# The first x tiles by transposing loads, and one gate earlier in TensorE's order, in a gated mix of two attention blocks

## The chip, the cores and the metric

The kernel runs on one core of a Trainium2 chip. The metric is the device time of one execution in microseconds (us), lower is better; three executions were timed and their median counts.

## The reference

One input x (2048 positions by 1024 features, bfloat16) goes through two attention blocks A and B, each with 32 heads of 32 features and its own weights, and the two results are mixed by a gate:

```python
g = sigmoid((x * gate_w).sum(-1, keepdims=True))
qkv = x @ wqkv                       # per block
# A: linear attention
pq, pk = phi(q), phi(k)              # phi(t) = where(t > 0, t + 1, exp(t)) + 1e-6
o = (pq @ (pk.T @ v)) / (pq @ pk.sum(positions) + 1e-6)
# B: each position attends to 8 positions, itself and 7 before it, 2 apart
o = softmax(q . k[pos - 2 w] / sqrt(32)) @ v[pos - 2 w],  w = 0..7
out = g * (oA @ A_wo) + (1 - g) * (oB @ B_wo)
```

B's own x is not used; both blocks read A's.

## The kernel before

**Tiles and pairs.** The positions are split into the even and the odd ones, 1024 each, since B looks back in steps of two. Each half has 8 row tiles of 128 positions, so there are tiles 0 to 15. A *pair* is two tiles of the same half, four apart: pair 0 is tiles 0 and 4, pair 1 tiles 1 and 5, pair 2 tiles 2 and 6, pair 3 tiles 3 and 7; pair 4 is tiles 8 and 12, pair 5 tiles 9 and 13, and so on (`tile_of`). x is needed with its features on the partitions, as `xT`.

**Products.** Most projections are made by a *group* (class `Group`): two row tiles by 1024 columns as a two by two block product with seven block products in place of eight (`m1` to `m7`). Each block product is a run of 128x128 by 512 matmuls in one line, L264; the operands that are sums of blocks are made beforehand on VectorE (DVE): `Weights.sums` (L131 to L134) for weights, `xsums` (L100 to L103) for x, the last of which overwrites a part of xT in place. ScalarE (ACT) copies partial results out of PSUM (L273), DVE adds them (L246).

**Queues.** The order of TensorE (PE) and of SyncE (SP), which issues nearly all loads and stores, is the order of the program text; ACT and DVE are ordered by a scheduler. SP issues its transfers one behind the other, and a store waits there until what it stores has been written.

**The start.** B's values come first, because attention reads them back from DRAM (`V_d`). The loads in SP's order: tile 0 of x plainly, into `xr` (L191), three of the four quarter loads of the first 512 columns of B's value weights `W` (`vb_load`, L184; the first quarter goes over ACT's queue), tile 4 of x plainly, tiles 1 and 5 by a transposing load straight into xT (`xt_load`, L90), the four quarters of the second 512 columns, then tiles 2, 6, 3 and 7 by transposing loads. All loads named here have 256 KB.

Meanwhile PE runs 14 matmuls on a zeroed tile (`warm_up`, L467), whose result nothing reads. `vb_plain(0, 1)` then makes the values of pairs 0 and 1 with ordinary products, tiles in the order 0, 4, 1, 5: eight matmuls (L520, psum tile K) over the eight feature chunks for the first 512 columns of each tile, and then the second 512 columns of all four. Before tile 0's first matmul stand the eight PE transposes of tile 0 (L476, with an identity `ident` built on GpSimd (POOL)), and before its seventh those of tile 4; ACT and DVE each copy half of the result into xT (L478).

After each tile's first half stands its `gate` (L456): eight matmuls of xT with one column, gate_w, into one column of the psum tile `gps`. `gate` for pairs 2 to 7 stands at written places between groups. All sixteen columns must be there at `gate_end`, which comes behind gates(6, 7) and value group 4.

Behind the plain products the program reads as follows (value groups of pairs 2 to 5 are `vb_group`; `run` issues a group; `defer` and `later` put work a number of products later):

```python
    vb_plain(0, 1)
    x_loads(4, 5)
    ws, xs = wvB.sums(), xsums(2)
    gates(2)
    ...
    later(2, lambda: gates(3))
    run(lambda: vb_group(2), 0)
    x_loads(6, 7)
    run(lambda: vb_group(3), 0)
    gates(4, 5)
    run(lambda: vb_group(4), 0)
    gates(6, 7)
    gate_end()
```

`x_loads(4, 5)` issues the transposing loads of tiles 8, 12, 9 and 13 on SP; ahead of them in SP's queue stand the four stores of V for pairs 0 and 1 (L502), each of which waits for ACT's last casts of these values. Value group 3 reads pair 3, value group 4 reads pair 4.

**The rest** (from about 47 us on) is the k and q groups, attention of B in pieces as side work between the products, A's k and v groups, A's q products with the linear attention, and the output products.

Of the kernel before, what the change touches and what calls it, by code (L numbers as in the profile page):

```python
# [9 lines left out]
ALU = mybir.AluOpType  # L10
AX = mybir.AxisListType
BF16 = mybir.dt.bfloat16
FP16 = mybir.dt.float16
F32 = mybir.dt.float32
P = 128
# [11 lines left out]
def kernel(  # L27
# [11 lines left out]
    nc = tc.nc  # L39
    ctx.enter_context(tc.manual_schedule(engines={mybir.EngineType.PE, mybir.EngineType.SP}))  # L40
    x = A_x[0]
    S, D = x.shape
# [10 lines left out]
    def xrows(t):  # L53
        return xpar[t // 8, (t % 8) * P:(t % 8 + 1) * P, :]

    consts = ctx.enter_context(tc.tile_pool(name="consts", bufs=1))
# [7 lines left out]
    ering = ctx.enter_context(tc.tile_pool(name="ering", bufs=4))  # L64
    smallp = ctx.enter_context(tc.tile_pool(name="smallp", bufs=4))
    ofp = ctx.enter_context(tc.tile_pool(name="ofp", bufs=3))
    ps_pj = ctx.enter_context(tc.tile_pool(name="ps_pj", bufs=1, space=bass.MemoryType.PSUM))
# [13 lines left out]
    xT = [xp.tile([P, 8, 2, 512], BF16, name="xT", tag=f"x{p}") for p in range(2)]  # L81
# [5 lines left out]
    def xt_load(t):  # L87
        p, j = divmod(t, 8)
        hf, c = divmod(j, 4)
        nc.sync.dma_start_transpose(out=xT[p][:, :, hf, c * P:(c + 1) * P], in_=xrows(t))  # L90

    def xsums(pair):
        p, c = divmod(pair, 4)
        sl = slice(c * P, (c + 1) * P)
        a11, a21 = xT[p][:, 0:4, 0, sl], xT[p][:, 0:4, 1, sl]
        a12, a22 = xT[p][:, 4:8, 0, sl], xT[p][:, 4:8, 1, sl]
        s1, s2, s4 = (SS[p][:, k, :, sl] for k in range(3))
        s3 = xT16[p][:, 0:4, 1, sl]
        tt = nc.vector.tensor_tensor
        return [lambda: tt(out=s1, in0=a21, in1=a22, op=ALU.add),  # L100
                lambda: tt(out=s2, in0=s1, in1=a11, op=ALU.subtract),
                lambda: tt(out=s4, in0=a12, in1=s2, op=ALU.subtract),
                lambda: (tt(out=s3, in0=a11, in1=a21, op=ALU.subtract), ready.add(pair))]  # L103
# [55 lines left out]
    def col_weights(src, col0, nn, pool=None):  # L159
# [3 lines left out]
        for j in range(2):  # L163
# [8 lines left out]
    W = wp.tile([P, 8, D], BF16, name="W", tag="W")  # L172
    T = tp.tile([P, 3, 4, 512], FP16, name="T", tag="T")
    T3v = kqp.tile([P, 4, 512], FP16, name="T3v", tag="kq")
    bview = B_wqkv.rearrange("(k p) n -> p k n", p=P)
    ident = consts.tile([P, P], BF16, name="ident")
    nc.gpsimd.memset(ident[:], 0.0)
    nc.gpsimd.affine_select(out=ident[:], in_=ident[:], compare_op=ALU.not_equal, fill=1.0, base=0,
                            pattern=[[1, P]], channel_multiplier=-1)
    gw = consts.tile([P, 8], BF16, name="gw")  # L180
    nc.gpsimd.dma_start(out=gw[:], in_=gate_w.rearrange("(k p) -> p k", p=P))

    def vb_load(k, j, q=nc.sync):
        q.dma_start(out=W[:, 2 * k:2 * k + 2, 512 * j:512 * j + 512],  # L184
                    in_=bview[:, 2 * k:2 * k + 2, 2 * D + 512 * j:2 * D + 512 * j + 512])

    xr = {}

    def xr_load(t):
        xr[t] = ering.tile([P, D], BF16, name="xr", tag="e")  # L190
        nc.sync.dma_start(out=xr[t][:], in_=xrows(t))  # L191
    vb_load(0, 0, nc.scalar)
    xr_load(0)
    vb_load(1, 0)
    vb_load(2, 0)
    vb_load(3, 0)
    xr_load(4)
    for t in (1, 5):
        xt_load(t)
    for k in range(4):  # L200
        vb_load(k, 1)
# [4 lines left out]
    def x_loads(*pairs):  # L206
        for pair in pairs:
            for i in range(2):
                xt_load(tile_of(pair, i))
# [30 lines left out]
    last_dve = [None]  # L240
# [154 lines left out]
    def defer(products, ops, gap=1):  # L395


        deferred.append([state["now"] + products, list(ops), gap])
# [3 lines left out]
    def later(products, f):  # L402
        tasks.append([state["now"] + products, f])
# [23 lines left out]
    def run(make, rate, *after, last=False):  # L427


        g, p = make(), state["prev"]  # L430
        g.after = after
        g.last = last
        for q, f in [(g, g.m1), (g, g.m2)] + ([(p, p.m3)] if p else []) + [(g, g.m6)] \
                + ([(p, lambda: end_of(p))] if p else []) + ([(g, g.m5), (g, g.m7)] if last else [(g, g.m7), (g, g.m5)]):
            f()
            side(rate, q.nk // 4)
        state["prev"] = g
# [7 lines left out]
    def tile_of(pair, i):  # L445
        return (pair // 4) * 8 + (pair % 4) + 4 * i
# [5 lines left out]
    def gate(t):  # L452
        p, j = divmod(t, 8)
        hf, c = divmod(j, 4)
        for kc in range(8):
            nc.tensor.matmul(gps[:, t:t + 1], lhsT=xT[p][:, kc, hf, c * P:(c + 1) * P], rhs=gw[:, kc:kc + 1],  # L456
                             start=kc == 0, stop=kc == 7)
# [7 lines left out]
    def warm_up(n):  # L465
        for _ in range(n):
            nc.tensor.matmul(gps_tile[:, 1, 0:256], lhsT=warm[:, 0:P], rhs=warm, start=True, stop=True)  # L467

    def transpose(t):
        p, j = divmod(t, 8)  # L470
        hf, c = divmod(j, 4)
        for k0, tag, copy in ((0, "X1", nc.scalar.copy), (4, "Y1", nc.vector.tensor_copy)):
            tps = ps_pj.tile([P, 512], F32, name="tps", tag=tag)
            tps = tps.bitcast(BF16)[:, 0:512].rearrange("p (k n) -> p k n", k=4)
            for k in range(4):
                nc.tensor.transpose(tps[:, k, :], xr[t][:, (k0 + k) * P:(k0 + k + 1) * P], ident[:])  # L476
            with tc.high_priority():
                last_dve[0] = copy(out=xT[p][:, k0:k0 + 4, hf, c * P:(c + 1) * P], in_=tps).ins  # L478


    def v_tiles(name):
        if name == "va":
            return [tring.tile([P, H, 32], BF16, name=name, tag="t") for _ in range(2)]
        vs = [tring.tile([P, H, 33], BF16, name=name, tag="t") for _ in range(2)]
        for v in vs:
            nc.gpsimd.memset(v[:, :, 32:33], 1.0)  # L486
        return vs

    def v_final(vs, by_chunk=False):
        def final(i, j, ps, add):  # L490
            if by_chunk:
                out_ = vs[i][:].rearrange("p (c a h) e -> p a c h e", c=4, a=2)[:, j, :, :, 0:32]
                rs = lambda ap: ap.rearrange("p (c h e) -> p c h e", c=4, e=32)
            else:
                out_ = vs[i][:, 16 * j:16 * j + 16, 0:32]
                rs = lambda ap: ap.rearrange("p (h e) -> p h e", e=32)
            acc(out_, rs(ps), None if add is None else rs(add))
        return final

    def vb_store(vs, pair, i):  # L500
        t = tile_of(pair, i)
        nc.sync.dma_start(out=V_d[t // 8][(t % 8) * P:(t % 8 + 1) * P, :],  # L502
                          in_=vs[i][:].rearrange("p h e -> p (h e)"))
# [5 lines left out]
    def vb_plain(*pairs):  # L509


        vs = {pair: v_tiles("va") for pair in pairs}
        tiles = [(pair, i) for pair in pairs for i in range(2)]

        def ps_of(pair, i):
            return ps_pj.tile([P, 512], F32, name="K", tag="XY"[i] + str(pair % 2))

        def mm(ps, pair, i, j, kc):
            p, c = divmod(pair, 4)
            nc.tensor.matmul(ps[:], lhsT=xT[p][:, kc, i, c * P:c * P + P],  # L520
                             rhs=wvB.W[:, kc, 512 * j:512 * j + 512], start=kc == 0, stop=kc == 7,
                             skip_group_check=True)
        for pair, i in tiles:
            ps = ps_of(pair, i)
            for kc in range(8):
                if (pair, i) == tiles[0] and kc in (0, 6):
                    transpose(tile_of(pair, kc // 6))
                mm(ps, pair, i, 0, kc)
            gate(tile_of(pair, i))
            v_final(vs[pair], True)(i, 0, ps[:], None)  # L530
        tiles = tiles[2:] + tiles[:2]
        ps = {t: ps_of(*t) for t in tiles}
        for k in range(4):
            for t in tiles:
                for kc in (2 * k, 2 * k + 1):
                    mm(ps[t], *t, 1, kc)
                if k == 3:
                    pair, i = t
                    v_final(vs[pair], True)(i, 1, ps[t][:], None)
                    vb_store(vs[pair], pair, i)  # L540
# [312 lines left out]
        return Group(operands, final, nk=8, scale=sc)  # L853


    warm_up(14)

    wkB, wqB, wqA = {}, {}, {}

# [10 lines left out]
    def load_q(nn, delay=8):  # L870
        return load_col(wqB, B_wqkv, 0, nn, delay=delay)
# [4 lines left out]
    def gates(*pairs):  # L876
        for pair in pairs:
            for i in range(2):
                gate(tile_of(pair, i))
    vb_plain(0, 1)  # L880
    x_loads(4, 5)
    ws, xs = wvB.sums(), xsums(2)
    gates(2)
    with tc.issue_after(last_dve[0]):
        for f in (ws[0], ws[1], xs[0], xs[1], ws[2], xs[3], ws[3], xs[2]):
            f()
    later(2, lambda: gates(3))
    defer(2, xsums(3) + xsums(0))
    run(lambda: vb_group(2), 0)
    x_loads(6, 7)  # L890
    defer(1, xsums(4) + xsums(1))
    run(lambda: vb_group(3), 0)
    load_k(0, 13)()
    load_q(0, 20)()
    gates(4, 5)
    defer(2, xsums(5))
    run(lambda: vb_group(4), 0)
    gates(6, 7)
# [101 lines left out]
```

## Time and profile before

| | |
|---|---|
| median of 3 executions | 460.67 us (460.46 to 460.70) |
| the profiled execution, its own time | 460.67 us |
| its span in the trace, first to last instruction | 458.9 us |
| mean granted clock of TensorE | 0.999 |
| PE busy | 446.0 us, 97% of the span |
| PE weight loads, DVE, ACT, POOL busy | 216.0, 282.9, 237.1, 60.8 us |
| moved by DMA | 51.61 MB |

All places in time are microseconds from the span's start. A row of the timeline has start, duration, engine, line, operation, output and inputs with shapes, and how many instructions were merged into it; in brackets, how long the engine was idle before it, and what ended that. "SPq" is SP's queue: the duration there is that of issuing, not of the transfer. "To landing" is from the start of issuing until the transfer's semaphore tells of its end. Matmuls are pipelined: a 512-column one is shown with 379 ns while the next one starts 216 ns later.

### The profile page before, as it was taken

Reading aid. Unit: us, or ns where it says so; the run is one execution under the profiler, and the core shown is the slowest. Engines: PE = TensorE matmul, PEld = TensorE weight load, DVE = VectorE, ACT = ScalarE, POOL = GpSimd, SP = SyncE. Lnnn points to the kernel's source line nnn. Section 1 sums busy time; section 2 is a strip of 40 time slices with the busy share of each in tenths; the row PEclk is TensorE's granted clock in tenths of the full one; section 3 lists DMA queues with packets and bytes.
Section 4 is the critical chain, followed back from the end, with each engine's and each line's share of the span. In section 5 each row is a group of like instructions: output and inputs, shape, how many; then the busy total and the mean of one; then the engine's idle time right before and its main releaser. Section 6 shows DMA issues by size and latency. Waiting matters only on the chain.

```text
span 458.9 us, 11765 instructions
## 1 busy us (share of the span) xinstructions
PE 446.0 (97%) x5070; PEld 216.0 (47%) x5070; DVE 282.9 (62%) x452; ACT 237.1 (52%) x345; POOL 60.8 (13%) x119
## 2 busy tenths in 40 slices
PE   6999999998999999999999999999999999999996
PEld 3455444444444444444445444445554444444444
DVE  0456768669748387484774846669777973256112
ACT  2234357557476484673855847536676544222221
POOL 8100000000000000000000000007686313000000
PEclk9999999999999999999999999999999999999999
DMA  8899911790301703007030066391229772695111
GB/s 219 149 227 246 297 18 71 204 193 3 99 4 38 155 1 101 1 26 165 5 98 4 24 135 189 109 244 47 71 74 216 169 172 91 146 219 129 48 46 46
DMA packets 111955, 51.61 MB, mean 112 GB/s; under 512 B 75552, under 2 KB 107552, under 8 KB 111904
## 3 DMA queue, kind: packets, MB, share of 16 engines
q1 hardware_dynamic: 111600, 50.61, 46.2%
q8 instruction: 39, 0.64, 0.6%
q10 hardware_dynamic: 272, 0.26, 0.2%
q14 instruction: 12, 0.10, 0.1%
q0 software_dynamic: 32, 0.00, 0.1%
HBM read 26.22 MB, written 16.78 MB: 94 GB/s over the span
## 4 chain that ended last, share of the span: by engine, by line
PE 90%; ACT 6%; DMA 1%; DVE 0%; SPq 0%; issue 0%; ACTq 0%; DVEq 0%
PE X L264 42%; PE Y L264 28%; PE Q L661 9%; PE K L520 3%; ACT PT L701 3%; PE o L712 2%; PE oA L618 2%; ACT eA L545 2%; PE s L696 1%; DMA xr<-in_A_x_dram 1%; PE kps L579 1%; ACT tA L244 1%; PE o L717 1%; PE Y L299 1%; ACT U2s L273 1%; PE gps L456 1%
## 5 line engine op out<-in xcount | busy, mean ns | idle before, releaser
L264 PEld LDWEIGHTS <-xT 128*128 128x128 bf16 (+1 forms) x352 | 33.0, 98 | 39.6 <-issue 1.8
L264 PE MATMUL X<-T,SS 128*128 128x512 f16 x176 | 45.3, 380 | 0.7 <-ACT U2s L273 0.7
L264 PEld LDWEIGHTS <-WS 128*128 128x128 bf16 (+1 forms) x288 | 28.1, 98 | 33.6
L661 PE MATMUL Q<-xT,WS 128*128 128x512 bf16 x192 | 43.7, 379 | 0.0
L264 PE MATMUL X<-SS,TS 128*128 128x512 f16 x144 | 37.0, 379 | 3.9 <-ACT U2s L273 3.9
L273 ACT COPY U4s<-X 128x512 f32<-128x512 f32 x40 | 23.4, 584 | 32.9 <-PE X L264 32.8
L486 POOL MEMSET vA<- 128x32 bf16 x16 | 4.0, 250 | 268.3 <-DVE eA L548 144.9
L264 PE MATMUL Y<-W,xT 128*128 128x512 bf16 (+1 forms) x152 | 39.0, 379 | 0.0
L264 PEld LDWEIGHTS <-SS 128*128 128x128 f16 x264 | 24.3, 98 | 29.7 <-issue 2.8
L701 ACT ACTIVATE PT<-s 128x2048 bf16<-128x2048 f32 x16 | 29.9, 1869 | 15.1 <-PE s L696 15.0
L264 PE MATMUL Y<-xT,WS 128*128 128x512 bf16 (+1 forms) x144 | 37.0, 379 | 0.0
L264 PEld LDWEIGHTS <-TS 128*128 128x128 f16 x216 | 20.5, 98 | 29.0 <-issue 5.9
L702 DVE TENSOR_TENSOR PT<-PT,maskp 128x2048 bf16<-128x2048 bf16 x16 | 19.6, 1224 | 22.1 <-ACT PT L701 22.1
L273 ACT COPY M1s<-X 128x512 f32<-128x512 f32 x40 | 23.6, 589 | 11.5 <-PE X L264 10.4
L661 PEld LDWEIGHTS <-WS 128*128 128x128 bf16 x192 | 18.3, 98 | 20.1
L273 ACT COPY U2s<-X 128x512 f32<-128x512 f32 x40 | 23.3, 583 | 8.2 <-PE X L264 8.2
L264 PEld LDWEIGHTS <-oT 128*128 128x128 bf16 (+1 forms) x176 | 17.2, 98 | 20.5
L629 POOL TENSOR_TENSOR obA<-ofv,rec 128x512 bf16<-128x512 f32 x22 | 25.7, 1187 | 0.9
L724 DVE COPY nB<-o 128x1024 f32<-128x1024 f32 x16 | 19.5, 1220 | 6.0 <-ACT rB L723 6.0
L723 ACT ACTIVATE rB<-o 128x1024 f32<-128x1024 f32 x16 | 16.4, 1025 | 12.3 <-DVE oB L730 9.5
L264 PE MATMUL X<-W,xT 128*128 128x512 bf16 x88 | 22.7, 380 | 0.0
L264 PE MATMUL X<-T,oS 128*128 128x512 f16 x96 | 22.7, 379 | 0.0
(140 smaller groups left out, 766.7 us busy)
## 6 DMA issues: line engine op xcount, KB each, us to landing
V_d<-va SPq DMA_DIRECT2D x16, 256.0 KB, 3.1
WS<-in_B_wqkv_dram SPq DMA_DIRECT2D x16, 256.0 KB, 4.2
W<-in_A_wqkv_dram SPq DMA_DIRECT2D x8, 512.0 KB, 6.0
vw<-V_d SPq DMA_DIRECT2D x16, 256.0 KB, 4.3
OB_d<-oB SPq DMA_DIRECT2D x16, 256.0 KB, 2.2
OA_d<-obA SPq DMA_DIRECT2D x16, 256.0 KB, 2.3
out_dram<-osb SPq DMA_DIRECT2D x30, 128.0 KB, 1.8
oT<-OB_d SPq DMA_DIRECT2D x12, 256.0 KB, 3.9
```

The costliest lines, as they stand in the source:

```text
L264: nc.tensor.matmul(ps[:], lhsT=lhsT, rhs=rhs, start=start and kc == 0, stop=kc == self.nk - 1, skip_group_check=True)
L273: nc.scalar.copy(out=s[:], in_=ps[:])
L520: nc.tensor.matmul(ps[:], lhsT=xT[p][:, kc, i, c * P:c * P + P], rhs=wvB.W[:, kc, 512 * j:512 * j + 512], start=kc == 0, stop=kc == 7, ski ...
L545: nc.scalar.activation(out=e, in_=t, func=ACT.Exp)
L618: nc.tensor.matmul(o[:, k, 132 * j:132 * j + 132], lhsT=es[i][:, j, k * P:(k + 1) * P], rhs=KVz[:, nn + 4 * j, :], start=True, stop=True)
L629: nc.gpsimd.tensor_tensor(out=ob[:, k:k + 2], in0=of[:, k:k + 2, :, 0:32], in1=rec[:, k:k + 2].broadcast_to([P, 2, 8, 32]), op=ALU.mult)
L661: nc.tensor.matmul(ps[:], lhsT=w.W[:, kc, j * P:j * P + P], rhs=xT[p][:, kc, i, :], start=kc == 0, stop=kc == 7, skip_group_check=True)
L701: nc.scalar.activation(out=PT[:], in_=s[:], func=ACT.Exp, scale=SCALE)
L702: nc.vector.tensor_tensor(out=PT[:], in0=PT[:], in1=maskp[:, None, :].broadcast_to([P, 4, 512]), op=ALU.mult)
L712: nc.tensor.matmul(o[32 * g:32 * g + 32, 2 * b, cols], lhsT=vw[rows, j, 4 * ch + g, :], rhs=PT[rows, g, cols], start=True, stop=True)
L723: nc.scalar.activation(out=rB[:], in_=o[:, 1:4:2, :], func=ACT.Ln)
L724: nc.vector.tensor_copy(out=nB[:], in_=o[:, 0:4:2, :])
```

## The change

Four edits, all in the first 35 us:

1. Tiles 0 and 4 of x are loaded by transposing loads straight into xT, as the others are. Tile 0's goes first on SP, tile 4's follows the three weight quarters. `transpose`, `xr`, the identity on POOL, 16 PE transposes and 4 copies on ACT and DVE go.
2. `warm_up` has 24 matmuls in place of 14 at the start, and three more stand before the third, fifth and seventh matmul of tile 0.
3. The sums for group 2 on DVE are no longer ordered behind the last copy of the transposes. DVE's order there becomes: first, second and third weight sum, first sum of x, fourth weight sum, the other three sums of x. Before, it was: first weight sum, first sum of x, second weight sum, second sum of x, third and fourth weight sum, and the last two sums of x.
4. `gates(4)` moves from behind value group 3 to ahead of it; `gates(5)` stays behind it.

Everything else has the same instructions in the same order on every engine and queue. Nothing of attention is in the diff.

```diff
-    ident = consts.tile([P, P], BF16, name="ident")
-    nc.gpsimd.memset(ident[:], 0.0)
-    nc.gpsimd.affine_select(out=ident[:], in_=ident[:], compare_op=ALU.not_equal, fill=1.0, base=0,
-                            pattern=[[1, P]], channel_multiplier=-1)
...
-    vb_load(0, 0, nc.scalar)
-    xr_load(0)
-    vb_load(1, 0)
-    vb_load(2, 0)
-    vb_load(3, 0)
-    xr_load(4)
-    for t in (1, 5):
+    vb_load(0, 0)
+    xt_load(0)
+    for k in range(1, 4):
+        vb_load(k, 0)
+    for t in (4, 1, 5):
         xt_load(t)
...
-    def transpose(t):
-        p, j = divmod(t, 8)
-        hf, c = divmod(j, 4)
-        for k0, tag, copy in ((0, "X1", nc.scalar.copy), (4, "Y1", nc.vector.tensor_copy)):
-            tps = ps_pj.tile([P, 512], F32, name="tps", tag=tag)
-            tps = tps.bitcast(BF16)[:, 0:512].rearrange("p (k n) -> p k n", k=4)
-            for k in range(4):
-                nc.tensor.transpose(tps[:, k, :], xr[t][:, (k0 + k) * P:(k0 + k + 1) * P], ident[:])
-            with tc.high_priority():
-                last_dve[0] = copy(out=xT[p][:, k0:k0 + 4, hf, c * P:(c + 1) * P], in_=tps).ins
...
-                if (pair, i) == tiles[0] and kc in (0, 6):
-                    transpose(tile_of(pair, kc // 6))
+                if (pair, i) == tiles[0] and kc in (2, 4, 6):
+                    warm_up(3)
                 mm(ps, pair, i, 0, kc)
...
-    warm_up(14)
+    warm_up(24)
...
-    with tc.issue_after(last_dve[0]):
-        for f in (ws[0], ws[1], xs[0], xs[1], ws[2], xs[3], ws[3], xs[2]):
-            f()
+    for f in (ws[0], ws[1], xs[0], xs[1], ws[2], xs[3], ws[3], xs[2]):
+        f()
...
     run(lambda: vb_group(2), 0)
     x_loads(6, 7)
+    gates(4)
     defer(1, xsums(4) + xsums(1))
     run(lambda: vb_group(3), 0)
     load_k(0, 13)()
     load_q(0, 20)()
-    gates(4, 5)
+    gates(5)
```

More of the change, by code (lines that the diff above doesn't have):

```diff
@@ L175, with vb_load @@
     bview = B_wqkv.rearrange("(k p) n -> p k n", p=P)
-    ident = consts.tile([P, P], BF16, name="ident")
-    nc.gpsimd.memset(ident[:], 0.0)
-    nc.gpsimd.affine_select(out=ident[:], in_=ident[:], compare_op=ALU.not_equal, fill=1.0, base=0,
-                            pattern=[[1, P]], channel_multiplier=-1)
     gw = consts.tile([P, 8], BF16, name="gw")
     nc.gpsimd.dma_start(out=gw[:], in_=gate_w.rearrange("(k p) -> p k", p=P))
[L183 to L191, printed above, removed]
-    vb_load(0, 0, nc.scalar)
-    xr_load(0)
-    vb_load(1, 0)
-    vb_load(2, 0)
-    vb_load(3, 0)
-    xr_load(4)
-    for t in (1, 5):
+    def vb_load(k, j):
+        (nc.scalar if (k, j) == (0, 0) else nc.sync).dma_start(out=W[:, 2 * k:2 * k + 2, 512 * j:512 * j + 512],
+                          in_=bview[:, 2 * k:2 * k + 2, 2 * D + 512 * j:2 * D + 512 * j + 512])
+    vb_load(0, 0)
[3 more added lines that the diff above has]
+    for t in (4, 1, 5):
         xt_load(t)
```

## The prediction

> **What bounds the kernel now.** The page first: it says which engine sets the time.
>
> ```profile
> PE 446.0 (97%) x5070; PEld 216.0 (47%) x5070; DVE 282.9 (62%) x452; ACT 237.1 (52%) x345; POOL 60.8 (13%) x119
> PE   6999999998999999999999999999999999999996
> ```
>
> TensorE (PE) is busy 97% of the span; only the first and the last of the 40 slices show holes. So every microsecond by which PE's stream starts later, or stands still, is a microsecond of the time. The chain of waits, cut to the start, shows what holds PE there (start, duration, what):
>
> ```profile
> 2.67 6.10 DMA xr<-in_A_x_dram
> 8.77 0.05 issue
> 8.82 0.62 PE tps L476 x8
> 9.44 0.43 PE K L520 x2
> 9.87 0.18 PE gps L456 x8
> 10.05 1.75 PE K L520 x8
> ```
>
> The chain runs through the load of row tile 4 (issued 2.67, landed 8.77), its eight transposes, the last two matmuls of tile 0, tile 0's gate, and then PE without a break. The timeline gives PE's start instruction by instruction (start, duration, and in brackets the idle time before it and what ended it):
>
> ```profile
> 1.20 3.05 PE L467 MATMUL gps<-KVacc 128*128 128x256 bf16 x14 [1.20 <-DVE KVacc L170]
> 4.16 0.62 PE L476 MATMUL tps<-ident,xr 128*128 128x128 bf16 x8
> 5.23 1.04 PE L520 MATMUL K<-W,xT 128*128 128x512 bf16 x4 [0.45 <-ACT xT L478]
> 6.99 0.59 PE L520 MATMUL K<-W,xT 128*128 128x512 bf16 x2 [0.72 <-DMA W<-in_B_wqkv_dram]
> 8.82 0.62 PE L476 MATMUL tps<-ident,xr 128*128 128x128 bf16 x8 [1.24 <-DMA xr<-in_A_x_dram]
> ```
>
> Tile 4's first matmul starts at 9.91, which is 1.14 us after its load landed. Next the same view of SP, the queue that issues the loads:
>
> ```profile
> 0.74 0.39 SPq L191 DMA_DIRECT2D xr<-in_A_x_dram  x1
> 1.19 1.44 SPq L184 DMA_DIRECT2D W<-in_B_wqkv_dram  x3
> 2.67 0.47 SPq L191 DMA_DIRECT2D xr<-in_A_x_dram  x1
> 3.18 5.33 SPq L90 DMA_TRANSPOSE xT<-in_A_x_dram  x2
> 24.18 11.99 SPq L90 DMA_TRANSPOSE xT<-in_A_x_dram  x8
> ```
>
> The eight transposing loads from 24.18 on are those of pairs 4 to 7; the first two are tiles 8 and 12, which make pair 4. Last, PE around the place to which the change moves pair 4's gate:
>
> ```profile
> 24.92 0.54 PE L456 MATMUL gps<-gw,xT 128*128 128x1 bf16 x16
> 25.33 1.02 PE L264 MATMUL X<-T,SS 128*128 128x512 f16 x4
> 27.05 1.03 PE L264 MATMUL X<-T,SS 128*128 128x512 f16 x4
> 27.91 1.03 PE L264 MATMUL X<-W,xT 128*128 128x512 bf16 x4
> 33.96 0.94 PE L456 MATMUL gps<-gw,xT 128*128 128x1 bf16 x32
> 34.76 1.02 PE L264 MATMUL X<-W,xT 128*128 128x512 bf16 x4
> ```
>
> and the landing of tile 12, from the answer for its line cut to its one issue, at 25.56:
>
> ```profile
> DMA to landing us min/median/max: 4.2/4.2/4.2
> ```
>
> The same answer for tile 8, issued at 24.18, has 4.5. So tile 8 lands at about 28.7 and tile 12 at 25.56 + 4.23 = 29.79.
>
> **Part 1, gates(4) moved.** PE takes its instructions in the written order. The change puts the 16 gate matmuls of pair 4 ahead of value group 3, whose first matmul runs at 27.91. They read tiles 8 and 12, which are not there until 28.7 and 29.79. In the kernel before, the same 16 stood behind group 3 at 33.96, four microseconds after both had landed, and waited for nothing. Queued behind them is all of PE, and behind PE the evictions of ACT and DVE and V's stores on SP. Nothing covers it. The price: PE comes to gate(8) near 27.9, waits for 28.7, does it, waits for 29.79, does gate(12), and goes on. Eight weight loads with eight narrow matmuls that nothing could prefetch take about 0.40 us (the load rows of gate(0): it starts at 9.49, the next matmul's load at 9.89). Group 3 starts at 29.79 + 0.04 + 0.40 = 30.23, that is 2.32 late. What is saved at the old place: 32 gate matmuls take 33.96 to 34.76 = 0.80 there, 16 take 24.92 to 25.33 = 0.41, so 0.39 comes off. **Net +1.93 us.** Both sides move with PE, for the loads of pair 4 are issued behind V's first four stores, which wait for casts that follow PE. An earlier or later start therefore doesn't change this stall. Bounds: with the quickest landing among the 14 such loads (4.1) it is +1.8; with the slowest (6.5) +4.2. I take 4.23, the row of this very load.
>
> Would the stall be given back? Behind 35 us the chain is PE with short stretches of ACT and DVE, all set off by PE itself; no DMA stands in it that a late PE would find ready. So it stays.
>
> **Part 2, the start.** Two plain loads of x (tiles 0 and 4) with 16 PE transposes, 2 ACT copies (0.59 each) and 2 DVE copies (0.42 each) go; two transposing loads come. What counts is when tile 4's matmuls start, 9.91 before; from there on PE's order is the same up to the gates of part 1. Gone is the 1.14 us between tile 4's landing and its first matmul. Against it the loads: the plain transfers between 4.11 (tile 0's load landed; PE's weight load for its first transpose starts at 4.15) and 8.77 are five of 256 KB, 0.93 us each. The eight transposing loads of 256 KB land from 24.18 + 4.5 to 34.28 + 4.1, seven gaps in 9.7 us, 1.38 each. So each exchange costs 0.45: tile 4 lands at 8.77 + 0.90 = 9.67. Further, the first of them holds SP 1.45 us (the first of the two from 3.18) in place of 0.39, so the weight loads are issued 1.06 later. That costs nothing as long as the DMA engines have work, and 1.06 if they run dry. Their busy share by microsecond (windows of the trace) is 0.26 from 1 to 2, 0.73 from 2 to 3 and 0.83 or more from there to 10, so I take 0.2, near the lower end. Tile 4 lands at 9.87 and its matmul starts at 9.92. **Net 0.0 us**, bounds -0.2 and +0.9 from the issue alone.
>
> The Trainium skill, page "Advanced Engine Details and Errata", section X-Bar Transpose (TRN2), says that transposing DMAs are as fast as ordinary ones. The rows above say otherwise (1.38 against 0.93); by the rule alone tile 4 would land at 8.77, the start come 1.1 us sooner, and the time be 461.5.
>
> With nothing of PE's to hide: the 24 warm-up matmuls. 14 took 3.05 us (218 ns each for 256 columns, half the later rate of 216 ns for 512), so ten more end between 5.3 and 6.5. From the late end, 8 matmuls (1.73), nine more warm-ups at the later rate (0.97) and the gate (0.2) end at 9.4, before tile 4 is there. They are hidden with 0.5 us to spare, and would show were tile 4 to land at 8.8.
>
> **Edits without a price.** Tiles 1 and 5 land at 11.25 and 12.6; needed at 11.85 and 13.8. The second half of the weights follows by 0.93 steps (13.6 to 16.4), needed from 15.7 to 20.9; tiles 2, 6, 3, 7 by 21.9, the last needed at 24.7. The tightest is tile 1 with 0.6. On POOL the identity (0.21 + 0.30) goes, and the gate vector's load is issued half a microsecond sooner. On DVE two of the three weight sums that stood behind the wait for tile 6 now stand ahead of it; the last of this group of sums ended at 23.70 and PE loads its result at 25.97, so nothing moves there. On SP one of the three transposing loads that now follow each other will be held as tile 5's is (5.33 for the two from 3.18, so 3.88 for the second), and the second half of the weights, queued behind it, is issued up to 2 us later: near 10.5, which with the 3.2 us that its first load took to land is 13.7 again. The attention code is the same on both sides of the diff.
>
> **The sum.** The profiled execution took 460.67 (span 458.9, and 1.8 around it) and is also the median. 460.67 + 1.93 + 0.0 = **462.6 us**. About 0.2% (0.9 us) is what a measurement of this kernel can tell from no change.
>
> **Rivals.**
> Transposing loads that cost no more than plain ones here (10%): tile 4 lands at 8.77 and its matmul starts at 8.82, 1.09 sooner; the stall stays: 460.67 + 1.93 - 1.09 = 461.5, within the 0.2%; a late end of the warm-ups would take back up to 0.6. For it: tile 1 (3.18 + 6.5) landed only 0.9 behind tile 4. Against: the 1.38 of eight in a row.
>
> Late start (9%): tile 0's load, now the first and a transposing one, takes 6.5 us from its issue as tiles 1 and 5 did, lands at 7.24 instead of 4.11, and all behind it slips: tile 4 at 7.24 + 4.66 + 0.45 = 12.35, the start +2.5, the time up to 465.1. Against: tiles 1 and 5 had six and seven loads ahead of them.
>
> The clock falls back (7%). In the stall PE is idle some 0.8 and 0.9 us; the start has short waits too. If the rate halves as in the first 3.05 us, half of that, 1.5 us, is lost: 464.1. Against: 1.24 us of idle time before 8.82, after which the matmuls ran at 216 ns each. The Trainium skill, "TensorE: Matmul & The Clock Gate", Part 1, puts the idle window after which the rate halves at about 3.4 us; no row here shows a wait that long.
>
> Faster (4%): the start comes forward by more than the gates cost. To be faster by 0.9 the first matmul of tile 4 would have to come at 9.91 - 1.93 - 0.92 = 7.06, so tile 4 land by 7.0, where before even the plain load landed at 8.77. At a landing of 6.5 the time is 459.2. Only a DMA queue that runs much quicker without the plain x loads does that, and no row shows one.
>
> **How the numbers follow.** The forecast has 70%. Slower by over 0.2%: 70 + 9 + 7 = 86%; same 10%; faster 4%. The range goes from the case of quick transposes, 461.5, to the forecast with the clock's loss or a late start, with some room for a slower landing in the stall: 464.7.
>
> **What would show it.** Right: in the timeline after, the gate's row behind group 2 has idle time of 1.5 to 2 us in front, ended by a DMA of xT; value group 3 starts 2.3 late against tile 4's start; the later gate row has 16 matmuls; PE's order and gaps behind it are as before. Tile 4's first matmul stands between 9.7 and 10.8. Wrong: no wait there (tiles 8 and 12 landed early), or a start that moves by more than a microsecond, or new waits at tiles 1 and 5.

## The result and the profile after

The changed kernel took 462.98 us (median of 4 executions, 462.49 to 463.25), the kernel before 460.69 (4 executions, 460.46 to 461.02): a ratio of 1.0048, 95% interval 1.0031 to 1.0065. The change makes the kernel slower, by 0.3 to 0.65%. The profiled execution after took 463.25, with a span of 461.5 against 458.9 before.

The page of the changed kernel, lines of busy time and of PE's 40 slices:

```profile
PE 448.1 (97%) x5073; PEld 217.6 (47%) x5073; DVE 282.4 (61%) x450; ACT 235.9 (51%) x343; POOL 59.4 (13%) x117
PE   8989999998999999999999999999999999999996
```

PE has 3 matmuls more (19 warm-ups came, 16 transposes went) and is still the bound. The first slice fills (6 to 8), the third falls from 9 to 8: a slice is 11.5 us, and the third holds the moved gate.

The chain of waits after, cut to the first 36 us (start, duration, what):

```profile
3.90 5.75 DMA xT<-in_A_x_dram
9.64 0.05 issue
9.69 1.90 PE K L497 x8
...
23.96 1.35 SPq L90
25.36 4.19 DMA xT<-in_A_x_dram
29.55 0.05 issue
29.60 0.35 PE gps L444 x8
29.95 0.89 PE X L252 x4
```

There are now two loads in it. The first is tile 4's, at the same place as before: landed at 9.64, first matmul 0.05 later. The second is new: tile 12's, which lands at 29.55 and releases its gate, and behind it value group 3. The timeline of PE shows both stretches (start, duration, what; in brackets the idle time in front). First the start:

```profile
1.20 4.85 PE L455 MATMUL gps<-KVacc 128*128 128x256 bf16 x24 [1.20 <-DVE KVacc L170]
5.89 0.59 PE L497 MATMUL K<-W,xT 128*128 128x512 bf16 x2
6.32 0.49 PE L455 MATMUL gps<-KVacc 128*128 128x256 bf16 x3
7.30 0.59 PE L497 MATMUL K<-W,xT 128*128 128x512 bf16 x2 [0.49 <-DMA W<-in_B_wqkv_dram]
9.25 0.34 PE L444 MATMUL gps<-gw,xT 128*128 128x1 bf16 x8
9.69 1.90 PE L497 MATMUL K<-W,xT 128*128 128x512 bf16 x8
```

Tile 4 starts at 9.69 against 9.91: 0.22 sooner. The only wait of note ahead of it is 0.49 for a weight quarter. Then the gate:

```profile
26.84 1.03 PE L252 MATMUL X<-T,SS 128*128 128x512 f16 x4
28.58 0.35 PE L444 MATMUL gps<-gw,xT 128*128 128x1 bf16 x8 [0.70 <-DMA xT<-in_A_x_dram]
29.60 0.35 PE L444 MATMUL gps<-gw,xT 128*128 128x1 bf16 x8 [0.67 <-DMA xT<-in_A_x_dram]
29.82 1.02 PE L252 MATMUL X<-W,xT 128*128 128x512 bf16 x4
35.85 0.54 PE L444 MATMUL gps<-gw,xT 128*128 128x1 bf16 x16
36.26 1.02 PE L252 MATMUL X<-W,xT 128*128 128x512 bf16 x4
```

Two waits on xT, one for each tile of pair 4. Value group 3 starts at 29.82 in place of 27.91, and value group 4, behind the now shorter gate row, at 36.26 in place of 34.76. So 1.50 us of the loss stand at 36 us: 1.72 for the gate, less 0.22 from the start.

The span, however, is 2.6 us longer. The other 1.1 come late, where both kernels have the same program. Half of it shows at one place, in B's attention; the row of the kernel before, then that of the changed one:

```profile
289.95 0.22 PE L712 MATMUL o<-PT,vw 64*32 64x56 bf16 x8 [0.32 <-issue]
```

```profile
292.00 0.23 PE L689 MATMUL o<-PT,vw 64*32 64x57 bf16 x11 [0.89 <-issue]
```

PE waits here for nothing that the trace shows, 0.32 us in one profile and 0.89 in the other. At this place, between the products `o` and the next group's, the profiles of the experiments below have 0.23 to 1.78, among them 0.40 (gate put back), 0.71 (gate two products later), 0.67 (the changed kernel again), 1.33 (gate put back, fewer warm-ups) and 1.78 (the kernel before with the extra warm-ups). So the gap varies from profile to profile, and it can be wide without the moved gate. That coming late widens it is not ruled out: it is at most 0.71 in the six profiles in which PE gets there before 290.6 us, and 0.46 to 1.78 in the eight in which it gets there later. The second profile of the changed kernel lost 1.90 by group 4 and 2.2 in its whole span (461.1 against 458.9). What sets these late increments was not found.

Some executions of several kernels, the kernel before among them (17 of 93), have a mean granted clock under 0.998 and take some 2 us longer; below they are said to have lost clock, and their share is given where it matters.

### The profile page after: what moved, and what is told of

The parts are those of the page before. It is cut to its first block, busy times and chain, and to the rows that moved or that the text cites. A ratio compares the mean times of both kernels' runs of the same rounds, so it can differ in the third digit from the quotient of the medians.

```text
span 461.5 us, 11765 instructions
## 1 busy us (share of the span) xinstructions
PE 448.1 (97%) x5073; PEld 217.6 (47%) x5073; DVE 282.4 (61%) x450; ACT 235.9 (51%) x343; POOL 59.4 (13%) x117
## 4 chain that ended last, share of the span: by engine, by line
PE 85%; ACT 6%; DMA 3%; SPq 2%; POOL 1%; DVE 1%; issue 1%; ACTq 0%; DVEq 0%; POOLq 0%
PE X L252 39%; PE Y L252 26%; PE Q L638 9%; ACT PT L678 3%; PE K L497 2%; PE o L689 2%; DMA xT<-in_A_x_dram 2%; ACT eA L522 2%; PE s L673 1%; PE oA L595 1%; PE kps L556 1%; DMA oT<-OA_d 1%; ACT tA L232 1%; POOL obA L606 1%; PE o L694 1%; PE Y L287 1%
```

## The experiments

The theory: the loss is the wait of pair 4's gate for tiles 8 and 12; the new start is even. The rivals: the start has a price of its own (transposing loads, warm-ups); or the granted clock falls in the waits.

### The two halves of the change

**The changed kernel with the gate put back** behind value group 3:

```diff
     x_loads(6, 7)
-    gates(4)
...
-    gates(5)
+    gates(4, 5)
```

> The changed kernel with pair 4's gate back behind value group 3 (gates(4, 5) there); its start stays as changed. Theory (the wait at the moved gate is the whole loss, the start is even): no wait of PE for a load of xT around 27.7, value group 3 starts at 27.7 (0.2 before that of the kernel before), time 460.4 to 460.7. Rival (the new start or what follows from it costs something late in the kernel, where the changed kernel's profile has about 1.1 us more than the moved gate explains): 461.0 to 461.8, with the surplus after 285 us.

Measured: 461.13 us (460.85 to 461.61, 12 executions) against 461.24 for the kernel before on the same chip (32 executions); ratio 0.9984, interval 0.9969 to 1.0000. The start by itself is even or a trifle quicker: of its 12 executions none lost clock, where 7 of the 32 of the kernel before did, and the other 25 of these have a median of 461.14. The time is above the 460.4 to 460.7 that I expected, and so is that of the kernel before on this chip.

**The kernel before with the gate ahead alone**, the other half:

```diff
     x_loads(6, 7)
+    gates(4)
...
-    gates(4, 5)
+    gates(5)
```

> The kernel before with pair 4's gate alone moved ahead of value group 3; the start stays as before. Theory: the whole loss is here, PE waits twice for loads of xT (together 1.3 to 1.5 us of idle matmul time), value group 4 starts 1.7 to 1.9 late, time 462.4 to 463.0. Rival (the start has part of the loss): under 462.0.

Measured: 465.50 us (462.37 to 466.99, 9 executions), ratio 1.0062 (1.0032 to 1.0092). By the median this is more than the changed kernel lost, and more than expected. Four executions that kept their clock have a median of 463.33, 2.2 over those of the kernel before (461.14); the other five, at 465.50 to 466.99, lost clock as well. The profiled execution is one of these. Its PE timeline at tile 4's transposes and around the gate:

```profile
9.74 1.03 PE L476 MATMUL tps<-ident,xr 128*128 128x128 bf16 x8 [2.24 <-DMA xr<-in_A_x_dram]
30.78 0.35 PE L456 MATMUL gps<-gw,xT 128*128 128x1 bf16 x8 [0.39 <-DMA xT<-in_A_x_dram]
32.64 0.35 PE L456 MATMUL gps<-gw,xT 128*128 128x1 bf16 x8 [1.51 <-DMA xT<-in_A_x_dram]
32.86 1.49 PE L264 MATMUL X<-W,xT 128*128 128x512 bf16 x4
```

and its windows (stretch, its length, PE's busy time and instructions, granted clock, DMA share, GB/s):

```profile
8.00:12.00 4.00, 2.25 (x19) 0.67 1.03 189
12.00:16.00 4.00, 3.95 (x29) 0.90 1.09 302
32.00:36.00 4.00, 3.14 (x16) 0.66 1.10 204
36.00:40.00 4.00, 4.00 (x19) 0.91 1.38 175
```

The clock is granted at 0.66 in the four microseconds of the gate's wait and after, and group 3's first four matmuls take 1.49 us where they took 1.02 or 1.03. So the rival of the clock is a thing that happens, at the gate and, in the first two rows, at the start of this old kernel too. There the wait was for tile 4: its plain load landed at 9.70 in this profile, not at 8.77, and PE stood idle for 2.24 us ahead of its transposes.

**The kernel before with a plain delay** of 18 warm-up matmuls at the gate's new place, and no gate moved. It asks whether a loss of 2 us at this place is given back:

```diff
     x_loads(6, 7)
+    warm_up(18)
```

> The kernel before with 18 matmuls of 256 columns on a zeroed tile, whose result nothing reads, put ahead of value group 3, where the changed kernel has the moved gate: PE is late by 18 x 0.108 = 1.94 us with no wait for a load. Theory (a delay of PE there is passed on to the end, one for one): 460.7 + 1.9 = 462.4 to 462.8. Rival one (the later kernel gives some of it back): under 462.2. Rival two (being late costs more, at the instruction supply near 290 and the loads of the output stage near 350): 463.1 to 463.8.

Measured: 465.02 us (463.17 to 467.29, 12 executions), ratio 1.0065 (1.0041 to 1.0089). In its profile the delay is as set: the row starts at 30.63, group 3 at 32.59, 1.96 later. Of the 12 executions 7 kept their clock, with a median of 463.86, 2.7 over the kernel before; nothing of the delay is given back. My 462.4 to 462.8 was missed, for no execution is under 463.17; the second rival, that being late costs more than the delay itself, is nearer. Of the places that it names, the gap near 290 us is 0.77 in this profile for 0.32 before. Why it is 2.7 and not 2.0, and why 5 of 12 lost clock though the delay itself leaves PE no idle time, this run doesn't tell; in its profile the clock fell at the start (0.74 and 0.83 in the stretches from 8 to 16 us), where PE had waited 2.17 us for tile 4's load.

### Is the wait the price, or the place?

**The changed kernel with the gate two products later**, inside value group 3, where PE comes when the tiles are about to be there:

```diff
-    gates(4)
+    later(2, lambda: gates(4))
```

> The changed kernel with pair 4's gate two products later, behind the second product of value group 3 instead of ahead of the group; the gate is neither back in its old place nor ahead. Theory (the cost is the landing of tile 12 less the time at which PE comes there): PE comes at 29.4 and tile 12 lands at 29.6 to 30.2, so 0 to 0.7 us of waiting are left in place of 1.9; median 461.0 to 461.6. Rival (the place itself costs, whatever PE's time there): 462.5 or more.

**The changed kernel as it is**, on the same chip:

> The changed kernel as it is, beside the others on the same chip, for the granted clock over more executions. Theory: the start keeps the clock (nothing under 1.00 in 8 to 16 us), the two waits of together 1.4 to 2 us at the moved gate halve it in some executions, which then cost 1 to 2 us more than the others; median 462.8 to 464. Rival (only the start's waits touch the clock): all within 462.4 to 463.4.

Measured: 461.05 us (460.56 to 462.25, 12 executions) for the later gate, ratio 0.9991 (0.9977 to 1.0005); 462.99 (462.42 to 464.85, 8 executions) for the changed kernel, ratio 1.0044 (1.0024 to 1.0064); the kernel before 461.40 on this chip. Two products, 1.7 us of PE's time, take away 1.94 us. PE's rows at the gate, with the gate two products later:

```profile
28.75 1.03 PE L252 MATMUL Y<-W,xT 128*128 128x512 bf16 x4
29.62 0.65 PE L444 MATMUL gps<-gw,xT 128*128 128x1 bf16 x16
30.13 1.02 PE L252 MATMUL X<-W,SS 128*128 128x512 bf16 x3
```

No idle time is left in front of the 16 gate matmuls. The price was PE's arrival against the landing; the early place has no other that could be measured. In the changed kernel's second profile the waits are 0.29 and 1.20, group 3 starts at 30.21, and the loss at group 4 is 1.90, of which 0.08 is the start. Three of its 8 executions lost clock (3 of 12 with the four of the result), where none of the 24 with the same start and without the wait did.

**The changed kernel with the gate's waits filled** by warm-up matmuls, so that PE isn't idle there:

```diff
-    gates(4)
+    warm_up(7)
+    gate(tile_of(4, 0))
+    warm_up(7)
+    gate(tile_of(4, 1))
```

> The changed kernel with 7 warm-up matmuls of 0.11 us each ahead of tile 8's gate and 7 between it and tile 12's gate, so that PE works for about 1.5 us of its two waits. Theory (the waits set the place of group 3, and their idle time is what halves the clock in some executions): median as the clock-intact runs of the changed kernel, 462.7 to 463.1, and none at 464.5 or with a mean clock under 0.997. Rival (the clock is lost elsewhere): some still there.

Measured: 463.85 us (462.49 to 464.90, 10 executions), ratio 1.0049 (1.0032 to 1.0065). No execution lost clock, against 3 of 8: that points the expected way, on small numbers. The median is above what was expected: 2.5 over the kernel before on its chip, where the changed kernel without these fillers has 1.6 on another. The ratios, 1.0049 and 1.0044, are not apart. Its profile was a late one: pair 4's loads were issued from 24.50 on in place of 23.96, a wait of 0.23 was left ahead of tile 8's gate, group 4 started at 37.15 in place of 36.26, and the late gap is 1.28. As a remedy for the gate's wait it saves nothing, since the landing stays where it is.

### The start: what the warm-ups are worth

**The changed kernel with the 14 warm-ups of before** and without the triples:

```diff
-                if (pair, i) == tiles[0] and kc in (2, 4, 6):
-                    warm_up(3)
...
-    warm_up(24)
+    warm_up(14)
```

> The changed kernel with 14 warm-up matmuls in place of 24, and none between tile 0's matmuls. Theory (hidden behind the loads): tile 4's first matmul still at 9.6 to 9.8, matmuls at 216 ns from there, time as the changed kernel, 462.7 to 463.3. Rival (the extra warm-ups hold the matmul rate up over the waits): tile 4's and tile 1's matmuls at up to 430 ns, up to 1.5 us more, 464 to 464.5.

Measured: 464.60 us (462.92 to 466.59, 12 executions), ratio 1.0054 (1.0035 to 1.0074); 7 of the 12 lost clock. My expectation was wrong, the rival's right: in the profile tile 4's eight matmuls run at half rate, behind a wait of 1.69 us for the weights.

```profile
9.93 3.29 PE L497 MATMUL K<-W,xT 128*128 128x512 bf16 x8
```

The lost clock is not all of it, though, for the five executions that kept it have a median of 464.39. And this kernel also has the gate's wait, which the next version takes out.

**The same with the gate put back**, which leaves of the change only the transposing loads and the order of the sums:

```diff
-                if (pair, i) == tiles[0] and kc in (2, 4, 6):
-                    warm_up(3)
...
-    warm_up(24)
+    warm_up(14)
...
-    gates(4)
...
-    gates(5)
+    gates(4, 5)
```

> The changed kernel with the gate back behind value group 3 and without the ten extra warm-up matmuls and the three triples: of the change only the transposing loads and the order of the sums on DVE are left. Theory: the extra warm-ups are worth something at the start itself. Without them PE stands idle for some 2 us in all between 4 and 9.7, the granted clock falls in the stretch from 8 to 16 as it did in the changed kernel without them (0.67 and 0.90), and most executions lose about 2 us: median 462.3 to 464, ratio 1.002 to 1.006, over a third of the executions with a mean clock under 0.998. Rival: they are worth something only together with the wait of the moved gate, which is what made the changed kernel without them slow; with the gate at its old place the time is that of the changed start with them, 460.9 to 461.5, ratio 0.998 to 1.0005, and the clock stays whole.

Measured: 462.61 us (461.84 to 463.34, 7 executions) against 461.18; ratio 1.0023, interval 0.9998 to 1.0047; 6 of the 7 lost clock. The median is that of the theory; the interval just reaches no difference, and the one execution that kept its clock is the slowest of the seven. The start of this kernel in the timeline:

```profile
1.20 3.17 PE L455 MATMUL gps<-KVacc 128*128 128x256 bf16 x14 [1.20 <-DVE KVacc L170]
4.92 0.60 PE L497 MATMUL K<-W,xT 128*128 128x512 bf16 x2 [0.56 <-DMA xT<-in_A_x_dram]
7.56 2.49 PE L497 MATMUL K<-W,xT 128*128 128x512 bf16 x6 [2.03 <-DMA W<-in_B_wqkv_dram]
10.10 2.53 PE L497 MATMUL K<-W,xT 128*128 128x512 bf16 x8
```

and its windows:

```profile
4.00:8.00 4.00, 1.41 (x6) 1.00 1.17 219
8.00:12.00 4.00, 3.97 (x19) 0.57 0.93 185
12.00:16.00 4.00, 3.95 (x33) 1.00 1.15 283
```

The first two matmuls run at the full rate (0.60 for both). PE then waits 2.03 us for the weights, and the next six take 2.49, the eight of tile 4 2.53 in place of 1.90: the clock is granted at 0.57. With the warm-ups back (the gate put back), the ten more at the start and the first triple fill much of the same hole, 1.34 us of waiting are left, and the clock stays at 1.00 in the windows up to 40 us:

```profile
7.67 0.59 PE L497 MATMUL K<-W,xT 128*128 128x512 bf16 x2 [1.34 <-DMA W<-in_B_wqkv_dram]
```

By the medians against the kernel before of each chip, the start is at +1.43 without the extra warm-ups and at -0.11 with them. Not all of this difference is seen at the start: group 4 comes at 35.59 without them and at 34.91 with them, 0.68 apart, and the rest of the 1.6 us between the two spans (460.7 and 459.1) comes late, where the gap near 292 is 1.33 for 0.40.

The Trainium skill, "TensorE: Matmul & The Clock Gate", Part 1, has the rate halve after an idle window of about 3.4 us. These rows show it after 2.03 us of idle time and, at the gate of the kernel before, after 1.51; the measurement decides.

**The kernel before with the fillers alone**, that is, the extra warm-up matmuls that fill PE's waits:

```diff
+                if (pair, i) == tiles[0] and kc in (2, 4, 6):
+                    warm_up(5 if kc == 6 else 3)
...
-    warm_up(14)
+    warm_up(24)
```

> The kernel before with the changed kernel's warm-up matmuls alone: 24 at the start, 3 ahead of tile 0's third and fifth matmul, 5 ahead of tile 4's transposes. Theory (in some executions PE's waits in the start halve the granted clock for some microseconds, and the extra matmuls prevent it): no execution with a mean granted clock under 0.998, none over 462.3, median 460.7 to 461.2. Rival (it is the transposes or the load order, not the idle time, that goes with the halved clock): a spread up to 464 as in the kernel before.

Measured: 462.71 us (461.03 to 465.29, 12 executions), ratio 1.0017 (0.9996 to 1.0037). I had this wrong, in the time and in the clock, which 2 of the 12 lost. The fillers are in the way here, for with plain loads there are PE transposes behind them:

```profile
1.20 5.30 PE L467 MATMUL gps<-KVacc 128*128 128x256 bf16 x24 [1.20 <-DVE KVacc L170]
6.29 0.76 PE L476 MATMUL tps<-ident,xr 128*128 128x128 bf16 x8
11.21 1.89 PE L520 MATMUL K<-W,xT 128*128 128x512 bf16 x8
```

Tile 0's transposes move from 4.16 to 6.29, and tile 4's first matmul from 9.91 to 11.21, which is the 1.3 us of the median. A filler is free only where what follows it is later than it anyway. The profiled execution is one of the two that lost clock, and it kept it at the start: all windows up to 40 us read 1.00. The clock fell behind the late gap, which is 1.78 us here:

```profile
292.53 0.30 PE L714 MATMUL o<-PT,vw 64*32 64x57 bf16 x29 [1.78 <-issue]
```

```profile
292.00:296.00 4.00, 3.47 (x45) 0.66 0.19 70
```

So lost clock is not always the start's, and this run doesn't show that the fillers fail there.

**The kernel before, profiled once more:**

> The kernel before once more, for a profile beside these. Theory: tile 4's load lands between 8.7 and 10.1 and its first matmul starts 1.1 to 1.3 us later; if the granted clock falls, it does so between 8 and 16 us.

Measured: 461.49 us, span 459.7. PE's start in this second profile:

```profile
4.63 1.04 PE L476 MATMUL tps<-ident,xr 128*128 128x128 bf16 x8 [0.26 <-DMA xr<-in_A_x_dram]
5.91 2.74 PE L520 MATMUL K<-W,xT 128*128 128x512 bf16 x6 [0.25 <-ACT xT L478]
8.97 1.03 PE L476 MATMUL tps<-ident,xr 128*128 128x128 bf16 x8 [0.31 <-DMA xr<-in_A_x_dram]
```

and one of its windows:

```profile
8.00:12.00 4.00, 3.63 (x25) 1.00 1.09 228
```

The same eight transposes take 1.04 and 1.03 in place of 0.62, and six matmuls 2.74: PE runs at half its later rate until about 10 us, with hardly a wait, while the granted clock of the window reads 1.00. Tile 4 landed at 8.92, and its first matmul came at 10.75 instead of 9.91. So the one profile from which the prediction was made is a good start of this kernel, not the only one.

### Versions with another start

**The kernel before with tiles 0 and 4 worked off together**: tile 4's plain load goes ahead of three weight quarters, and each quarter is used for both tiles when it comes; two fillers before each later quarter.

```diff
     xr_load(0)
+    xr_load(4)
...
-    xr_load(4)
...
+        for k in range(4):
+            if k:
+                warm_up(2)
...
+            for pair, i in tiles[:2]:
+                if k == 0:
+                    transpose(tile_of(pair, i))
+                for kc in (2 * k, 2 * k + 1):
+                    mm(pp[pair, i], pair, i, 0, kc)
...
```

> The kernel before with another start: tile 4's plain load goes ahead of the three weight quarters, both tiles are transposed at once, their matmuls go quarter by quarter as the weights land (four per quarter, two warm-up matmuls ahead of each of the last three), and both gates stand ahead of the last quarter. Theory (the start is bound by the loads; whatever PE does while it waits for them is free): when the last quarter has landed, at about 8.8, only four matmuls are left, tile 1's first matmul comes at 9.8 to 10.4 instead of 11.84, time 1.4 to 2.0 under the kernel before, and with a busier PE the granted clock stays at 1.00 in 8 to 16 us. Rival (the gain is lost where the sums for group 2 wait for tiles 6 and 7, which land as before at 18.4 and 20.8): under 0.5.

Measured: 460.28 us (459.99 to 460.72, 12 executions) against 461.40, ratio 0.9978 (0.9969 to 0.9988), a gain, but less than expected: group 4 starts at 34.12, 0.64 sooner than before. The weights were there by 8.71; it was PE that came late, with tile 0's transposes at half rate (1.06 us) and the fillers now in its way.

**The same without fillers, and both tiles transposed first:**

```diff
+        for pair, i in tiles[:2]:
+            transpose(tile_of(pair, i))
         for k in range(4):
-            if k:
-                warm_up(2)
...
-                if k == 0:
-                    transpose(tile_of(pair, i))
```

> As the kernel with tiles 0 and 4 at once, but both tiles are transposed one behind the other ahead of the first matmul, and no warm-up matmuls stand between the quarters. Theory (in that kernel PE itself was late: the last quarter had landed at 8.71 and its four matmuls ran at 10.34): tile 1's first matmul at 9.9 to 10.4 instead of 11.2, median 459.0 to 459.8. Rival (without the extra matmuls the clock is lost as in the kernel before): clock-intact runs as said, but some at 461 to 463 with a mean clock under 0.997.

Measured: 459.43 us (458.76 to 460.06, 10 executions) against 461.32, ratio 0.9958 (0.9943 to 0.9972). It beats both kernels. Its start:

```profile
4.16 1.06 PE L476 MATMUL tps<-ident,xr 128*128 128x128 bf16 x8
5.47 0.84 PE L476 MATMUL tps<-ident,xr 128*128 128x128 bf16 x8 [0.25 <-ACT xT L478]
6.15 2.97 PE L520 MATMUL K<-W,xT 128*128 128x512 bf16 x12
8.96 0.54 PE L456 MATMUL gps<-gw,xT 128*128 128x1 bf16 x16
9.36 2.75 PE L520 MATMUL K<-W,xT 128*128 128x512 bf16 x11
```

From 6.15 on PE has no wait: with two tiles to work on, each weight quarter gives it twice the work while the next one travels. Group 4 starts at 33.15, 1.61 sooner than before. No execution of this and of the one before it, 22 in all, lost clock.

## Why the prediction was right, and where it was not

The time is the forecast's, 462.98 for 462.6. In the profile the two stages that the forecast reckoned with make 1.50 of the 2.6 us, and the other 1.1 came late, where it said that PE's gaps are as before. That the sum is so near is to this extent luck. By its own steps:

**Part 1, right.** The two waits are in front of the gate rows, both ended by a DMA of xT, 1.37 us in sum in one profile and 1.49 in the other, just under the 1.5 to 2 named. Tile 12 landed at 29.55 (29.79 was predicted), with 4.19 from its issue for the 4.23 taken. The later gate row takes 0.41, which saves the 0.39 reckoned. One term was too large: from tile 12's landing to group 3 it took 0.27 and 0.26 us, not 0.44, so the weight loads and narrow matmuls of a gate cost less than taken. Net: 1.72 and 1.82 in the two profiles and 1.94 between the medians with the gate early and two products later (1.81 among executions that kept the clock), for 1.93 predicted. It stays, too: a plain delay at this place came back at least in full.

**The remark that the stall doesn't change with the start, not tested apart.** In the two profiles the start differs by 0.3 us and the net by 0.1.

**Part 2, right in its sum, with luck in what it is made of.** The start is even: -0.22 in the first profile, +0.08 in the second, -0.11 between medians. Tile 4 landed between 9.6 and 10.2 in all seven profiles with this order of loads, around the 9.87 predicted; the 8.77 of the rival with quick transposes was not seen. But the plain load of the kernel before, against which it was set, doesn't land at 8.77 each time either: 8.92, 9.70 and 9.98 in three later profiles of that start, 10.08 with fillers. The sum compared a value at the lower end of a spread with an estimate in the middle of one. So it isn't shown that the exchange costs 0.45 a load.

The step that was short is "They are hidden with 0.5 us to spare", of the 24 warm-up matmuls. They are hidden, with about 0.2 to spare, since PE also waits for the second weight quarter (0.49 us in one profile, 1.31 in the other). But they are not without worth. Tile 1's first matmul, ahead of which all of this lies, comes at 13.26 and 12.67 in the two profiles without the extra warm-ups and at 11.6 to 12.2 in the five with them. In both of the former PE stood idle for long in one piece (1.69 and 2.03 us) and the clock fell. I counted a filler by its cover alone, and not by the idle time that it breaks up. The start of the change is even only with the warm-ups; how much each of its edits costs or gains was not taken apart further.

**The rival of the falling clock** had the mechanism right, and argued against itself from 1.24 us of idle time that did no harm in one profile. The single waits behind which, or at whose end, the clock fell in the 14 profiles are 1.51, 1.69, 1.78, 2.03, 2.17 and 2.24 us; behind those up to 1.50 (among them 1.50, 1.20 and 0.70 at the gate) it did not. In the changed kernel it befell 3 of 12 executions and left the median where the wait alone puts it; it befell 17 of 93 executions of the kernel before, which the forecast didn't reckon with on that side at all. The late start didn't come: tile 0 landed at about 4.9, not 7.24.

What stays open: why the kernel before with the gate ahead or with a delay lost clock so much more often (10 of 21) than alone (17 of 93), though in both profiles the clock fell at the start, which is the same; what else held back the executions that kept their clock without the extra warm-ups; and what lengthens the late gaps without a cause in the trace.

## What to carry to other kernels

A small step with inputs of its own is put where its inputs have landed when the engine comes to it: the same 16 narrow matmuls cost 1.9 us ahead of a group, and nothing that could be measured two products later. Dummy matmuls at the start are to be judged by two questions, whether the work behind them is late anyway and how long the idle time is that they break up; better than either is real work, here a second row tile for each weight load. Where a first load's landing decides, one profile gives one draw of it, and a second profile of the unchanged kernel is worth having before a difference under a microsecond is believed.

## What the hardware showed that was not expected

The rate of TensorE at the start is not settled by a fixed amount of warm-up: after the same 14 matmuls it was full by 4.2 us in one profile of the kernel before and still half at 9.8 in another, and in that stretch the granted clock of the profile reads 1.00, so that the spacing of the matmuls has to be read instead. Later it fell with six single waits of 1.51 to 2.24 us and with none up to 1.50; the two lie too near to each other for a limit to be read from this. It was then at half for some 3.4 us: a mean of 0.57 over 4 us is 3.4 us at half, which loses 1.7 us of a busy PE, and 0.66 and 0.91 over two such stretches come to the same. The Trainium skill, "TensorE: Matmul & The Clock Gate", Part 1, says that the length of the slow start differs from run to run; the two profiles agree, with a wider spread than the half microsecond either way that it gives for the transition.
